# Trainium2: reordering the end of the dense stage and of the last token pair, and operand sums moved to GpSimd, in a fused attention, dense and routed-expert kernel

## The chip, the cores and the metric

The kernel runs on one core of one Trainium2 chip. The metric is the device time of one execution in microseconds (us). The times of before are the median of three runs; the profile comes from one more execution, whose own time stands beside its span below. Engines are named PE (TensorE, matmuls), ScalarE or ACT, VectorE or DVE, GpSimd or POOL, and SyncE or SP, whose queue issues most of the DMAs.

## The reference

```python
def reference(q, k, v, moe..., moe2...):
    # attention: 4 batches, 8 heads, 576 positions, 64 per head;
    # heads 0-3 see the last 32 positions, heads 4-7 every 32nd
    x = attention(q, k, v)                       # 2304 x 512
    gate = 1.0 / (1.0 + np.exp(-(x @ w_gate)))   # w_gate, w_val: 512 x 1536
    x = (gate * (x @ w_val)) @ w_out             # w_out: 1536 x 512
    # routed experts: 8 of them, w1 512 x 1024, w2 1024 x 512
    do_compute = (x @ w_skip) > 0
    xc = x[do_compute]
    e_idx = np.argmax(xc @ w_gate2, axis=1)      # one expert a token
    for e in range(8):
        y[e_idx == e] = gate_w * (np.maximum(xc[e_idx == e] @ w1[e], 0.0) @ w2[e])
    out = x.copy(); out[do_compute] = xc + y
```

The attention's inputs are float32, and the products are held to float32 accuracy: the kernel splits an operand into a high half, rounded for the fast matmul, and a low half, the rest.

## The kernel before, in words

The 2304 tokens are six units of 384 (`UT`), taken in three pairs p = 0, 1, 2 (`NP`). There are four stages.

1. **Attention**, up to about 130 us of the span. Its output leaves in transposed tiles `x`.

2. **Dense stage**, about 131 to 397 us. Gate and value matrices are multiplied in `NC` = 12 chunks of weights (f), for each pair p, by a seven-product scheme for 2 x 2 blocks (Strassen-Winograd): sums of weight blocks (S1 to S4) meet sums of token blocks (T1 to T4). A `Block(f, p)` is one such set of seven products of six matmuls, 128 x 384 each; `mm3` (L593 to L595) makes a product of split operands from three matmuls: high x high, high x low, low x high. The partial sums stand in PSUM banks psA, psB, psC and psD. `period` is the order of one block: it is a generator whose steps mix the products of the block with the end of the block before (`prev`). At its start ScalarE copies psB of the block before into psC (`onto`, L632) and into a temporary (`keep`, L625), and the last products of that block add onto psC. VectorE adds psD onto temporaries (`add_d`, L639) and multiplies gate by value (L655, L658, L666, L670); DMAs store the results in the DRAM tensors `gts` (gT, gB), partly accumulating from GpSimd's queue (L644, L646).

   Work beside the blocks sits in job queues for VectorE ("D"), ScalarE ("A") and GpSimd ("P"). Each step of a period calls `background`, which takes jobs from each queue up to a credit (`RATES`, in us a step) by the jobs' given costs; `need` forces a job and those that it depends on when a product needs its operand. Jobs are: token sums (`combine`, L417; on VectorE for pair 2 in the kernel before), the high half (ScalarE, L429) and low half (VectorE, L433) of token operands, the conversion of weights from 64-bit to 32-bit floats (`convert`, VectorE's L460, L464, L469 and L489, ScalarE's L478), the weight sums (L520) and the split of weights (`split_w`: high halves `wh` on ScalarE, L534; low halves `wl` on VectorE, L537). `out_weights(i)` does the same for a chunk of w_out into a box `wof` and, for every second chunk, makes the weight sums (L576 to L585) and stores all of them in DRAM (wS, wA). The raw weights are fetched one after another in the order of the list `raws_left`; each finished conversion asks for the next (`more_raw`).

   In the last block the operands of the first output steps (`wt["A11", g]`, xt[2], xt[0], xt[1], `wt["A12", 0]`) are loaded and queued as split jobs, and the queues are emptied before `period(None, prev)` ends the last block.

3. **Output projection**, about 397 to 546 us: `NSTEP` = 63 steps k, 21 a pair, three for each of the seven products P1 to P7 in the order of `PROD`. Step k loads the token tile five steps ahead (`load_x`, L970) and weight tiles (`load_w`, L977); ScalarE casts the high half three steps ahead (L984), VectorE subtracts the low half two steps ahead (L992). `finish` splits the sums of a unit's half; `turn_back` turns them with matmuls into rows of tokens (PE L1085 and L1086, ScalarE's row copy L1087, VectorE's L1088 for the routing logits lp); `pick(u)` chooses each token's expert (L1115 to L1125, result oh_all) and stores its rows into the output; `place(u, rank_sums)` ranks the tokens of each expert with small matmuls (L1047 to L1050) and scatters rows to the experts' slots (xs). `at(k, generator, n)` puts n pieces of such work into step k. For the last pair, unit 4 is picked and placed, and unit 5 turned, picked and placed, in straight code after step 62, between the first tiles of expert 0 (`hide`, `hidden`, L1438 to L1442).

4. **Routed experts**, to the end: `hidden_wide` and `outputs_wide` for experts 1 to 7, and for expert 0 `hidden` and `outputs` (L1505 to L1514). GpSimd makes some low halves of expert weights there (L1168).

Instructions are issued in program order on each engine; tiles of one pool tag are reused in turn, and a tile's new writer waits for its old readers.

Of the kernel before, what the change touches and what calls it, by code (L numbers as in the profile page):

```python
# [16 lines left out]
ALU = mybir.AluOpType  # L17
# [6 lines left out]
def kernel(  # L24
# [14 lines left out]
    nc = tc.nc  # L39
    B, H, S, D = q.shape  # L40
# [370 lines left out]
    def combine(p, nm, eng, parts, cost):  # L411

        e = nc.gpsimd if eng == "P" else nc.vector
        for part in parts:
            def fn(part=part):
                x, y = (source(p, z)[:, part, :] for z in SUMS[nm])
                e.tensor_tensor(source(p, nm)[:, part, :], x, y, op=ALU.subtract)  # L417
            before = [sum_job[p, z] for z in SUMS[nm] if z[0] == "T"]
            sum_job[p, nm] = Job(eng, cost, fn, before)
# [317 lines left out]
    def run(steps, n=99):  # L737
        for _ in range(n):
            if next(steps, 0) == 0:
                return  # L740
# [150 lines left out]
    raws_left = []  # L891
    for f in range(2, NC):
        raws_left += [(f, "g"), (f, "v")] + [(i, "o") for i in outs_of[f - 1]]
    raws_left += [(NC - 1, "o")]

    def more_raw():
        if raws_left:
# [7 lines left out]
        operand(1, nm, WHOLE, 0.8, 0.9)  # L905
    split_w(1, *c1)
    for nm in ("T3", "T2", "T4"):
        combine(2, nm, "D", WHOLE, 0.95)
    for nm in OPS:
        operand(2, nm, WHOLE, 0.8, 0.9)  # L910
        if nm in ("T3", "T2", "T4"):
# [26 lines left out]
    def slab2(shape, dt, name):  # L938
        return late.tile(shape, dt, tag="slab2", bufs=NBIG, name=name)

    PROD = (("P1", "A11", "B11", "A"), ("P2", "A12", "B21", "A"), ("P6", "S2", "T2", "B"), ("P7", "S3", "T3", "D"),
            ("P5", "S1", "T1", "B"), ("P4", "A22", "T4", "D"), ("P3", "S4", "B22", "B"))
    NSTEP = NP * len(PROD) * NG
    xt = {}
    wt = {}
# [10 lines left out]
    def load_x(n):  # L956
        if not 0 <= n < NSTEP:
            return
        p, r = divmod(n, len(PROD) * NG)
        j, g = divmod(r, NG)  # L960
        src = gts[p, PROD[j][2], g]
        if n < 2 or (n - 2) % (NBIG + 1) == 0:
            get = (raw_w if n < 2 else
                   lambda shape, dt, name: keep.tile(shape, dt, tag="w3", bufs=2, name=name))
            xt[n] = [get([128, 2, UT], F32, f"xt{n}{c}") for c in range(2)]
            for c in range(2):
                nc.sync.dma_start(xt[n][c][:, 1, :], src[:, c, :])
        else:
            xt[n] = slab2([128, 2, 2, UT], F32, f"xt{n}")
            nc.sync.dma_start(xt[n][:, 1], src)  # L970
# [28 lines left out]
    for f, p in BL:  # L999
        if (f, p) == (0, 2):  # L1000
            for nm in OPS:
                for j in x_jobs[2, nm]:
                    need(j)
            weights(2, more_raw)
        if p == 0 and f > 1:
            if f + 1 < NC:
                weights(f + 1, more_raw)
            for i in outs_of[f]:
                out_weights(i, more_raw)
        if (f, p) == (NC - 1, 1):  # L1010
            for i in outs_of[f]:
                need(wo_jobs[i])
            for g in range(NG):
                load_w("A11", g)
            for n in (2, 0, 1):
                load_x(n)
            load_w("A12", 0)
        k = Block(f, p)
        for i, _ in enumerate(period(k, prev)):
            background(RATES)  # L1020
            if rest0:
                rest0.pop()()
            if (f, p, i) == (NC - 1, NP - 1, 0):
                for x in [wt["A11", g] for g in range(NG)] + [xt[2], xt[0], xt[1], wt["A12", 0]]:
                    split_job(x)
        prev = k
    for eng in "AD":
        while queue[eng]:
            need(queue[eng][0])
    for _ in period(None, prev):  # L1030
        pass
    for eng in "PAD":
        while queue[eng]:
            need(queue[eng][0])
# [7 lines left out]
    def rank_sums(oh, tag="Y"):  # L1042
        nb = oh.shape[1]
        pk = bank([RB, nb + 1, NE], tag)
        for m in range(nb):
            for mm in range(m):
                nc.tensor.matmul(pk[:, m, :], lhsT=ones, rhs=oh[:, mm, :], start=(mm == 0), stop=False)  # L1047
            nc.tensor.matmul(pk[:, m, :], lhsT=tri, rhs=oh[:, m, :], start=(m == 0), stop=True)
        for m in range(nb):
            nc.tensor.matmul(pk[:, nb, :], lhsT=ones, rhs=oh[:, m, :], start=(m == 0), stop=(m == nb - 1))  # L1050
        return pk
# [189 lines left out]
    def finish(u, a, sums, k, adds=None):  # L1241

        if k < NSTEP - 4:
            sh, sl = (raw_w([128, 2, UT], F32R, f"s{n}{u}{a}") for n in "hl")
        else:
            both = slab2([128, 2, 2, UT], F32R, f"s{u}{a}")
            sh, sl = both[:, 0], both[:, 1]
        splits[u, a] = sh, sl

        def highs(x):  # L1250
            for c in range(2):
                nc.scalar.copy(sh[:, c, :], x[c])

        def lows(x):
            for c in range(2):
                nc.vector.tensor_tensor(sl[:, c, :], x[c], sh[:, c, :].bitcast(F32), op=ALU.subtract)

        if adds:
            for c in range(2):
                nc.vector.tensor_tensor(adds[c], adds[c], sums[c], op=ALU.add)  # L1260
            at(k + 1, do(lambda: (highs(adds), after_act.append(lambda: lows(adds)))))
        else:
            highs(sums)
            if k + 1 < NSTEP:
                after_act.append(lambda: lows(sums))
            else:
                lows(sums)
# [9 lines left out]
    def at(k, gen, n=1):  # L1277
        side.setdefault(k, []).append((gen, n))
# [43 lines left out]
    for p in range(NP):  # L1322
        b, ua, ub = PER * p, 2 * p, 2 * p + 1
        last = p == NP - 1
        ta = [later(lambda u=ua, a=a: turn_back(u, a)) for a in range(2)]
        tb = [later(lambda u=ub, a=a: turn_back(u, a)) for a in range(2)]
        for k in range(8, 11):
            at(b + k, ta[0])
        for k in range(17, 20):
            at(b + k, tb[1])  # L1330
        if last:
            at(b + 20, ta[1], 4)
        else:
            for k in range(20, 23):
                at(b + k, ta[1])
        if last:
            break
        for k in range(23, 26):
            at(b + k, tb[0])
        for u, k0 in ((ua, 23), (ub, 27)):  # L1340
            g = later(lambda u=u: pick(u))
            for k in range(k0, k0 + 3):
                at(b + k, g, 3)
            g = later(lambda u=u: place(u, rank_sums(rst[u][1])))
            for k in range(k0 + 3, k0 + 6):
                at(b + k, g, 2)
# [21 lines left out]

    banks, keeps = {}, {}

    def unit(p, j, d, g):

        name, wn, xn, t = PROD[j]
        ps, w, x = banks[t][d], wt[wn, g], xt[PER * p + NG * j + g]
        for c in range(2):
            ds_ = slice(128 * d, 128 * d + 128)
            xhi, xlo = ((x[c][:, i, :] for i in range(2)) if isinstance(x, list) else (x[:, i, c, :] for i in range(2)))
            first, end = g == 0 and c == 0, g == NG - 1 and c == 1
            mm3(ps, w[:, 0, c, ds_].bitcast(F32R), w[:, 1, c, ds_].bitcast(F32R), xhi.bitcast(F32R), xlo.bitcast(F32R),
                first and name in ("P1", "P7"), end, True)  # L1380

# [15 lines left out]
    for p in range(NP):  # L1397
        for t in "ABD":
            banks[t] = [bank([128, UT], t) for d in range(2)]
        if p == 0:  # L1400
            for ps in banks["B"]:
                nc.tensor.matmul(
                    ps, lhsT=wt["A11", 0][:, 0, 0, 0:128].bitcast(F32R), rhs=xt[0][0][:, 0, :].bitcast(F32R),
                    start=True, stop=True)
        for j, (name, _, _, _) in enumerate(PROD):
            wide = name in ("P1", "P2")
            for g in range(NG):
                k = PER * p + NG * j + g
                ahead(k)
                flush(after_act)  # L1410
                two = [divmod(2 * g + i, NG) for i in range(2)] if wide else [(0, g), (1, g)]
                for d, x in two:
                    unit(p, j, d, x)
                    if name == "P1" and x == NG - 1:
                        nc.scalar.copy(banks["B"][d], banks["A"][d])
                for gen, n in side.get(k, ()):
                    run(gen, n)
            after(p, name, k)
# [152 lines left out]
    def hide(*fs):  # L1571
        for f in fs:
            hidden(f, w, pp, hts, 0, HEAD)()

    grab()
    grab()
    hide(0)
    evict = hidden(1, w, pp, hts, 0, HEAD)
    run(pick(NU - 2))
    run(turn_back(NU - 1, 0))  # L1580
    evict()
    run(place(NU - 2, rank_sums(rst[NU - 2][1])))
    run(pick(NU - 1))
    hide(2)
    evict = hidden(3, w, pp, hts, 0, HEAD)
# [168 lines left out]
```

## Time and profile before

| | us |
|---|---|
| median of 3 runs (lowest to highest) | 746.56 (746.31 to 746.75) |
| the profiled execution's own time | 746.6 |
| its span | 744.8 |
| PE busy | 708.6 (95%) |
| VectorE busy | 561.4 (75%) |
| ScalarE busy | 452.1 (61%) |
| GpSimd busy | 258.7 (35%) |

The profile's times count from the start of the span. A timeline row gives start, duration, engine, line, operation, the tile written and the tiles read, shape, and in square brackets the idle time of the engine ahead of the row with what ended it. A row of waits gives waiting engine, line and tile, then the releaser, then the sum of the waits in us, how many, and the longest. PE's granted clock stands in windows as a share of full speed: 1.00 is 2.4 GHz and 0.50 is 1.2 GHz.

### The profile page before, as it was taken

To read this page: it belongs to the slowest core of one execution; us is meant where nothing else is said; L and a number is where in the kernel's file an instruction comes from. 1 tells how busy PE (TensorE), PEld (TensorE's weight loads), DVE (VectorE), ACT (ScalarE), POOL (GpSimd) and SP (SyncE) were. 2 spreads that over 40 slices of the span, in tenths; PEclk is the share of its full clock that TensorE was granted. 3 is DMA by queue.
4 is the path that set the end of the run, shared out by engine and by line. 5 is a ranking of instruction groups with operands and counts; after the bars stand their busy time and mean duration, and the time that the engine had idled before them with its cause. 6 is when DMAs were issued, how large, how long until landed. Compare 5 with 4: busy or idle time off the path is not lost. (4 is left out here: it accounts for less than half of the span.)

```text
span 744.8 us, 14549 instructions
## 1 busy us (share of the span) xinstructions
PE 708.6 (95%) x4783; PEld 663.7 (89%) x4785; DVE 561.4 (75%) x1246; ACT 452.1 (61%) x1206; POOL 258.7 (35%) x289
## 2 busy tenths in 40 slices
PE   8999988999999999999988999999989999999992
PEld 5766666999999999999988999999989899999991
DVE  4799997989988888888866766677865666666650
ACT  5888986755555555555454856565645666676730
POOL 6677876021030211204042000402415644566611
PEclk9999999999999999999998999999998999999997
DMA  9999610397897888979599996779845577677610
GB/s 201 238 208 209 157 41 30 109 256 196 272 222 251 210 233 220 228 256 208 171 293 336 356 326 203 247 235 319 302 162 183 179 238 246 225 246 232 223 38 14
DMA packets 136858, 158.57 MB, mean 213 GB/s; under 512 B 60511, under 2 KB 105823, under 8 KB 136777
## 3 DMA queue, kind: packets, MB, share of 16 engines
q1 hardware_dynamic: 122072, 134.51, 58.4%
q0 software_dynamic: 11936, 19.66, 13.0%
q10 hardware_dynamic: 2768, 3.41, 1.3%
q8 instruction: 40, 0.66, 0.4%
q14 instruction: 42, 0.34, 0.2%
HBM read 103.49 MB, written 59.65 MB: 219 GB/s over the span
## 5 line engine op out<-in xcount | busy, mean ns | idle before, releaser
L644 POOL DMA_DIRECT2D gT<-sC x36 | 31.9, 1030 | 171.1 <-DVE sC L658 137.2
L301 ACT ACTIVATE sm<-psX,mx 96x128 f32<-96x128 f32 (+2 forms) x176 | 61.9, 376 | 10.0 <-DVE mx L295 7.9
L314 POOL TENSOR_TENSOR sm<-sm,rs 96x384 f32<-96x384 f32 (+2 forms) x64 | 55.5, 885 | 31.1 <-DVE rs L308 16.2
L984 ACT CAST xt<-xt 128x768 fp32r<-128x768 f32 (+1 forms) x74 | 53.9, 743 | 18.6 <-DMA xt<-gB 10.4
L992 DVE TENSOR_TENSOR xt<-xt 128x768 fp32r<-128x768 f32 (+1 forms) x74 | 60.4, 831 | 5.8 <-ACT xt L984 5.7
L639 DVE TENSOR_TENSOR u<-psD,u 128x384 f32<-128x384 f32 x70 | 38.6, 552 | 19.0 <-PE psD L595 18.7
L593 PE MATMUL psD<-xhT,wh 128*128 128x384 f32 x140 | 47.3, 338 | 1.5 <-DVE u L639 1.5
L595 PE MATMUL psA<-xhB,wl 128*128 128x384 f32 x140 | 47.0, 336 | 1.3 <-DVE wl L537 1.3
L595 PE MATMUL psD<-xhT,wl 128*128 128x384 f32 x140 | 47.4, 338 | 0.3 <-DVE wl L537 0.3
L594 PE MATMUL psD<-xlT,wh 128*128 128x384 f32 x140 | 47.2, 337 | 0.0
L593 PE MATMUL psA<-xhB,wh 128*128 128x384 f32 x140 | 46.8, 334 | 0.0
L595 PE MATMUL psB<-xhT,wl 128*128 128x384 f32 x140 | 46.8, 334 | 0.0
L594 PE MATMUL psA<-xlB,wh 128*128 128x384 f32 x140 | 46.8, 334 | 0.0
L593 PE MATMUL psB<-xhT,wh 128*128 128x384 f32 x140 | 46.8, 334 | 0.0
L594 PE MATMUL psB<-xlT,wh 128*128 128x384 f32 x140 | 46.8, 334 | 0.0
L632 ACT COPY psC<-psB 128x384 f32<-128x384 f32 x35 | 16.3, 465 | 43.4 <-PE psB L595 43.4
L1521 POOL DMA_INDIRECT out_dram<-xg x16 | 15.3, 957 | 77.2 <-DVE xg L1520 66.4
L625 ACT COPY u<-psB 128x384 f32<-128x384 f32 x70 | 33.9, 484 | 11.2 <-PE psB L595 10.9
L1119 POOL COPY row<-lm_all 128x8 f32<-128x8 f32 x18 | 6.9, 424 | 94.4 <-DVE lm_all L1115 94.4
L301 ACT ACTIVATION_READ_ACCUMULATOR sm<-psX,mx 96x1 f32 (+2 forms) x176 | 38.3, 218 | 0.0
L593 PE MATMUL psB<-xt,wtS 128*128 128x384 f32 x108 | 36.9, 341 | 0.0
L594 PE MATMUL psB<-xt,wtS 128*128 128x384 f32 x108 | 36.3, 336 | 0.6 <-DVE xt L992 0.6
(793 smaller groups left out, 2553.1 us busy)
## 6 DMA issues: line engine op xcount, KB each, us to landing
w1r<-in_moe_w_dram SPq DMA_DIRECT2D x28, 512.0 KB
w2r<-in_moe_w_dram SPq DMA_DIRECT2D x28, 512.0 KB
xt<-gT SPq DMA_DIRECT2D x30, 384.0 KB
gT<-u SPq DMA_DIRECT2D x54, 192.0 KB
xt<-gB SPq DMA_DIRECT2D x22, 384.0 KB
gT<-sC POOLq DMA_DIRECT2D x36, 192.0 KB, 5.9
gB<-sA SPq DMA_DIRECT2D x33, 192.0 KB
wg<-in_moe_w_gate_dram SPq DMA_DIRECT2D x12, 512.0 KB
```

The costliest lines, as they stand in the source:

```text
L301: nc.scalar.activation(sm[:n, w, 0:c], src[:, w, :], AF.Exp, bias=mx[:n, w:w + 1], accum_out=sums[:n, h, w:w + 1])
L314: nc.gpsimd.tensor_tensor(x, x, rs[:n, h, 0:m].rearrange("p (w o) -> p w o", o=1).to_broadcast([n, m, c]), op=ALU.mult)
L593: nc.tensor.matmul(ps, lhsT=whi, rhs=xhi, start=start, stop=False, skip_group_check=skip)
L594: nc.tensor.matmul(ps, lhsT=whi, rhs=xlo, start=False, stop=False, skip_group_check=skip)
L595: nc.tensor.matmul(ps, lhsT=wlo, rhs=xhi, start=False, stop=stop, skip_group_check=skip)
L625: nc.scalar.copy(self.tm[nm], self.ps["B"])
L632: nc.scalar.copy(ps, self.ps[src])
L639: nc.vector.tensor_tensor(self.tm[nm], self.ps["D"], self.tm[nm], op=ALU.add)
L644: nc.gpsimd.dma_start(dst, t, accum_op=ALU.add)
L984: nc.scalar.copy(h.bitcast(F32R), l)
L992: nc.vector.tensor_tensor(l.bitcast(F32R), l, h, op=ALU.subtract)
L1521: ins = nc.gpsimd.indirect_dma_start(out=out[:, :], out_offset=bass.IndirectOffsetOnAxis(ap=xg[t][:n, TW - 1:TW].bitcast(I32), axis=0), in ...
```

## The change

- `raws_left`: the last four raw weights are fetched in the order output chunk 9, gate 11, value 11, output chunk 10 and then output chunk 11; in block (10, 0) `out_weights(9)` is queued ahead of `weights(11)`, and chunk 10 behind it.
- The sums T3, T2 and T4 of pair 2 are made by GpSimd, whole tiles of 128 x 768, with a cost of 1.8 instead of 0.95 in the job queue.
- In the last block only the A11 tiles and xt[2] are queued as split jobs. The splits of xt[0], xt[1] and `wt["A12", 0]` stand between the steps of the closing period: after its first step, after three more and at its end. The bank copy of L632 comes ahead of them.
- The first product P1 of the output projection takes its k-slices in the order 2, 0, 1.
- The last pair's products: P4 ahead of P5 (`PRODS`). P4's finish (step 56) makes its additions and high halves at once. Unit 4 is turned back in steps 58 and 59 and picked in steps 60 to 62; unit 5's second half is turned in step 62. After step 62, `place(4)` follows the first `hide(0)`, ahead of `hidden(1)` and of unit 5's turn.

```diff
-    raws_left += [(NC - 1, "o")]
+    raws_left[-4:] = [raws_left[i] for i in (-2, -4, -3, -1)] + [(NC - 1, "o")]
...
     for nm in ("T3", "T2", "T4"):
-        combine(2, nm, "D", WHOLE, 0.95)
+        combine(2, nm, "P", WHOLE, 1.8)
...
+    PRODS = [PROD] * (NP - 1) + [PROD[:4] + (PROD[5], PROD[4]) + PROD[6:]]
...
         if p == 0 and f > 1:
+            if f == NC - 2:
+                out_weights(outs_of[f][0], more_raw)
             if f + 1 < NC:
                 weights(f + 1, more_raw)
-            for i in outs_of[f]:
+            for i in outs_of[f][f == NC - 2:]:
                 out_weights(i, more_raw)
...
-                for x in [wt["A11", g] for g in range(NG)] + [xt[2], xt[0], xt[1], wt["A12", 0]]:
+                for x in [wt["A11", g] for g in range(NG)] + [xt[2]]:
                     split_job(x)
...
-    for _ in period(None, prev):
-        pass
+    tail = period(None, prev)
+    for n, x in ((1, xt[0]), (3, xt[1]), (9, wt["A12", 0])):
+        run(tail, n)
+        high(x)
+        low(x)
...
-        if adds:
+        if adds and k == NSTEP - 7:
+            for c in range(2):
+                nc.vector.tensor_tensor(adds[c], adds[c], sums[c], op=ALU.add)
+            highs(adds)
+            after_act.append(lambda: lows(adds))
+        elif adds:
...
-        for k in range(17, 20):
-            at(b + k, tb[1])
-        if last:
-            at(b + 20, ta[1], 4)
-        else:
+        if not last:
+            for k in range(17, 20):
+                at(b + k, tb[1])
+        if not last:
             for k in range(20, 23):
                 at(b + k, ta[1])
         if last:
+            for k, n in ((16, 1), (17, 2)):
+                at(b + k, ta[1], n)
+            g = later(lambda: pick(ua))
+            for k in range(18, 21):
+                at(b + k, g, 3)
+            at(b + 20, tb[1], 4)
             break
...
-                    unit(p, j, d, x)
+                    unit(p, j, d, (x + 2) % NG if k < NG else x, x)
...
     hide(0)
+    run(place(NU - 2, rank_sums(rst[NU - 2][1])))
     evict = hidden(1, w, pp, hts, 0, HEAD)
-    run(pick(NU - 2))
     run(turn_back(NU - 1, 0))
     evict()
-    run(place(NU - 2, rank_sums(rst[NU - 2][1])))
     run(pick(NU - 1))
```

Three places where the order of instructions changes follow. The first is GpSimd's queue at the start of the dense stage; xT are token sums, the L644 rows are the accumulating stores of the first block. A piece of the difference:

```order
 L417 TENSOR_TENSOR xT_2256<-x_963,xT_2154 128x384
 L417 TENSOR_TENSOR xT_2364<-x_2029,x_1498 128x384 x2
-L644 DMA gT_00_86<-sC_2612 128x384
-L644 DMA gT_00_83<-sC_2612 128x384
-L644 DMA gT_00_89<-u_10_2533 128x384
+L417 TENSOR_TENSOR xT_2421<-x_2030,x_2029 128x768
+L417 TENSOR_TENSOR xT_2454<-x_2030,xT_2364 128x768
+L417 TENSOR_TENSOR xT_2474<-x_1499,xT_2454 128x768
```

The three sums of pair 2 are new in this queue and stand ahead of the first block's stores; on VectorE they stood right behind the two subtractions L537 of chunk 1.

The second is ScalarE at the end of the dense stage, from the gate's sigmoid of the last block on; xt and wtA are the tiles that come from DRAM. Before:

```order
L636 ACTIVATE sA_5210<-psA 128x384
L984 CAST xt_5073<-xt_5073 128x384
L984 CAST xt_5074<-xt_5074 128x384
L984 CAST xt_5077<-xt_5077 128x384
L984 CAST xt_5078<-xt_5078 128x384
L984 CAST wtA_5081<-wtA_5081 128x512
L632 COPY psC<-psB 128x384
L625 COPY u_112_5237<-psB 128x384
```

Now:

```order
L636 ACTIVATE sA_5210<-psA 128x384
L632 COPY psC<-psB 128x384
L625 COPY u_112_5227<-psB 128x384
L985 CAST xt_5073<-xt_5073 128x384
L985 CAST xt_5074<-xt_5074 128x384
L636 ACTIVATE sC_5240<-psC 128x384
L985 CAST xt_5077<-xt_5077 128x384
L985 CAST xt_5078<-xt_5078 128x384
L985 CAST wtA_5081<-wtA_5081 128x512
```

The bank copy and the addend's copy moved ahead of the five casts (L984, which is L985 in the changed file).

The third is PE after the last output step; L1438 to L1442 are a hidden tile of expert 0 (L1454 to L1458 in the changed file), L1085 the turn of unit 5 and L1048 the rank sums (L1054). Before, from the end of the first hidden tile on:

```order
L1442 MATMUL psY<-xx_6992,we03l 128x128
L1438 MATMUL psY<-xx_6992,we03h 128x256
L1438 MATMUL psY<-xx_6992,we00h 128x256
L1440 MATMUL psY<-xx_6992,we00l 128x128
L1438 MATMUL psY<-xx_6992,we01h 128x256
L1440 MATMUL psY<-xx_6992,we01l 128x128
L1438 MATMUL psY<-xx_6992,we02h 128x256
L1440 MATMUL psY<-xx_6992,we02l 128x128
L1442 MATMUL psY<-xx_6992,we03l 128x128
L1438 MATMUL psY<-xx_6992,we03h 128x256
L1085 MATMUL psY<-wri,s_7040 128x148
```

Now:

```order
L1458 MATMUL psY<-xx_7007,we03l 128x128
L1454 MATMUL psY<-xx_7007,we03h 128x256
L1054 LDWEIGHTS tri
L1054 MATMUL psY<-oh_all,tri 128x8
L1053 LDWEIGHTS ones
L1053 MATMUL psY<-oh_all,ones 128x8
```

The rank sums of unit 4 stood behind unit 5's turn and stand right behind the first hidden tile now.

## Rows read from the trace of the kernel before

**Rows 1.** The page, busy us, share of the span, instructions, per engine

```profile
PE 708.6 (95%) x4783; PEld 663.7 (89%) x4785; DVE 561.4 (75%) x1246; ACT 452.1 (61%) x1206; POOL 258.7 (35%) x289
```

**Rows 2.** PE's waits: releaser, sum in us, times, longest

```profile
PE psC L593 <- ACT psC L632: 4.2, 1, 4.2
...
PE psD L593 <- DVE u L639: 1.5, 1, 1.5
PE psY L1048 <- DVE oh_all L1125: 1.4, 1, 1.4
...
PE psB L594 <- DVE xt L992: 0.6, 1, 0.6
...
PE psD L595 <- DVE wl L537: 0.3, 1, 0.3
```

**Rows 3.** PE's timeline, end of the dense stage

```profile
388.29 0.33 PE L594 MATMUL psB<-xlT,wh 128*128 128x384 f32 x1
388.46 0.34 PE L595 MATMUL psB<-xhT,wl 128*128 128x384 f32 x1
393.00 0.69 PE L593 MATMUL psC<-xhB,wh 128*128 128x384 f32 x1 [4.21 <-ACT psC L632]
393.49 0.52 PE L594 MATMUL psC<-xlB,wh 128*128 128x384 f32 x1
...
398.61 0.41 PE L593 MATMUL psA<-xt,wtA 128*128 128x384 f32 x1
```

**Rows 4.** ScalarE's timeline, same place

```profile
391.95 0.62 ACT L984 CAST wtA<-wtA 128x512 fp32r<-128x512 f32 x1 [0.50 <-DMA wtA<-wA]
392.48 0.47 ACT L632 COPY psC<-psB 128x384 f32<-128x384 f32 x1
```

**Rows 5.** Windows: length, each engine's busy us, PE's clock, DMA share, GB/s

```profile
410.00:420.00 10.00, 10.00 (x62) 10.00 (x61) 7.25 (x12) 8.23 (x16) 0.00 (x0) 1.00 0.96 326
...
430.00:440.00 10.00, 9.98 (x61) 9.76 (x59) 6.51 (x10) 4.91 (x8) 0.00 (x0) 1.00 1.05 368
...
444.00:450.00 6.00, 5.84 (x36) 5.66 (x36) 5.48 (x14) 4.05 (x10) 0.00 (x0) 1.00 0.39 126
```

**Rows 6.** ScalarE's timeline, output projection

```profile
434.09 0.83 ACT L984 CAST xt<-xt 128x768 fp32r<-128x768 f32 x1 [2.39 <-DMA xt<-gB]
```

**Rows 7.** VectorE's timeline, ahead of block (11, 0)

```profile
364.95 0.43 DVE L460 TENSOR_SCALAR wof<-wo 128x512 int32<-128x512 int32 x1 [1.89 <-DMA wS<-wof]
```

**Rows 8.** VectorE's timeline, start of the dense stage

```profile
129.95 0.77 DVE L351 COPY x<-psY 128x108 f32<-128x108 f32 x2 [1.14 <-PE psY L339]
...
136.26 0.96 DVE L537 TENSOR_TENSOR wl<-stage,wh 128x768 fp32r<-128x768 f32 x1 [0.25 <-ACT wh L534]
137.59 1.22 DVE L537 TENSOR_TENSOR wl<-stage,wh 128x1024 fp32r<-128x1024 f32 x1 [0.37 <-ACT wh L534]
...
140.07 1.94 DVE L417 TENSOR_TENSOR xT<-x,xT 128x768 f32<-128x768 f32 x2
```

**Rows 9.** GpSimd's timeline, end of the attention stage

```profile
123.39 1.32 POOL L417 TENSOR_TENSOR xT<-x,xT 128x384 f32<-128x384 f32 x1
124.79 1.98 POOL L417 TENSOR_TENSOR xT<-x,x 128x384 f32<-128x384 f32 x2
```

**Rows 10.** Timelines of GpSimd and VectorE, 104 to 107 us

```profile
104.38 1.73 POOL L314 TENSOR_TENSOR sm<-sm,rs 96x384 f32<-96x384 f32 x2 [1.07 <-ACT kq L258]
...
104.13 0.51 DVE L433 TENSOR_TENSOR xlT<-xT,xhT 128x384 fp32r<-128x384 f32 x1
...
105.03 1.50 DVE L433 TENSOR_TENSOR xlT<-xT,xhT 128x384 fp32r<-128x384 f32 x1
```

**Rows 11.** PE's timeline, after the last output step

```profile
556.95 0.18 PE L1048 MATMUL psY<-oh_all,tri 128*128 128x8 bf16 x1 [1.41 <-DVE oh_all L1125]
```

**Rows 12.** Windows, same columns, expert 0

```profile
559.00:566.00 7.00, 7.00 (x27) 6.12 (x27) 2.71 (x10) 3.73 (x10) 4.53 (x10) 0.51 0.28 106
```

**Rows 13.** Waits of the DMA queue on SP, 382 to 444 us

```profile
SPq L970 <- PE psB L595: 8.5, 6, 2.6
```

More of the change, by code (lines that the diff above doesn't have):

```diff
@@ L960, in load_x @@
         j, g = divmod(r, NG)
-        src = gts[p, PROD[j][2], g]
+        src = gts[p, PRODS[p][j][2], g]
         if n < 2 or (n - 2) % (NBIG + 1) == 0:
@@ L1369, with unit @@
     banks, keeps = {}, {}
-    def unit(p, j, d, g):
-        name, wn, xn, t = PROD[j]
+    def unit(p, j, d, g, i):
+        name, wn, xn, t = PRODS[p][j]
         ps, w, x = banks[t][d], wt[wn, g], xt[PER * p + NG * j + g]
@@ L1376, in unit @@
             ds_ = slice(128 * d, 128 * d + 128)
-            xhi, xlo = ((x[c][:, i, :] for i in range(2)) if isinstance(x, list) else (x[:, i, c, :] for i in range(2)))
-            first, end = g == 0 and c == 0, g == NG - 1 and c == 1
+            xhi, xlo = ((x[c][:, z, :] for z in range(2)) if isinstance(x, list) else (x[:, z, c, :] for z in range(2)))
+            first, end = i == 0 and c == 0, i == NG - 1 and c == 1
             mm3(ps, w[:, 0, c, ds_].bitcast(F32R), w[:, 1, c, ds_].bitcast(F32R), xhi.bitcast(F32R), xlo.bitcast(F32R),
@@ L1404 @@
                     start=True, stop=True)
-        for j, (name, _, _, _) in enumerate(PROD):
+        for j, (name, _, _, _) in enumerate(PRODS[p]):
             wide = name in ("P1", "P2")
```

## The prediction

> **What bounds the kernel now.** I began with the page: PE is busy for 95% of the span, VectorE for 75% [rows 1]. So time can be gained only where PE waits or where its clock is down, and it is lost wherever PE is made to wait. The waits of PE, sorted by what ended them, name the places [rows 2]: 4.2 us once for the bank copy of L632, 1.5 us once for the addition of L639, 1.4 us once for oh_all of L1125.
>
> The 4.2 us stand at the end of the dense stage [rows 3]: PE's last matmul into psB starts at 388.46, the next one at 393.00, and then at half speed. From 393.49 to 398.61 sixteen matmuls follow one another at 0.32 us, where 388.29 to 388.46 shows 0.17. That is 16 x 0.15 + 0.3 (the first one, 0.49 instead of 0.17) = 2.7 us more. The place costs 4.2 + 2.7 = 6.9 us. ScalarE's timeline shows why [rows 4]: the copy stands behind five casts, each of which waits for a load from DRAM or for the one before it (391.95, after a wait of 0.50, is the last); it runs at 392.48 although its input was complete before 389.
>
> **The change, part by part.** All sums are against the profiled execution (span 744.8, its own time 746.6; the median of the runs, 746.56, is 0.04 below it). A difference below 0.2%, 1.5 us, can't be told from no change.
>
> *Bank copy first.* The copy and the addend's copy no longer stand behind casts that wait for DMA. At the place itself it leaves some 0.5 us (the eviction of 0.47 us in [rows 4] and its handover), so 6.9 - 0.5 = 6.4 us come free at 389. The question is whether they arrive at the end. The windows [rows 5] say no: the DMA engines are busy for a share of 0.96 to 1.05 in the stretches shown up to 440 (those around them, from 382 to 444, read alike) and 0.39 after 444. In that stretch ScalarE, two to three output steps ahead of PE, already waits 2.4 us at once for a tile [rows 6], and PE itself 0.6 us for one [rows 2]. An earlier PE reaches those tiles earlier, and they come no sooner. What can be kept is the free share, 10 x (1 - 0.96) = 0.4 us, and PE's own 0.6 us, which comes from the row copies that ScalarE has to do between PE's steps: 1.0 us. The bounds are 0 and 6.4; I take -1.0, since the row of the full DMA engines is the nearest.
>
> *Weight chunk 9 earlier.* VectorE's L460 at 364.95 had waited 1.89 us for the store of the previous box [rows 7]; behind it in VectorE's queue stands the addition on which PE's 1.5 us end [rows 2]. Now chunk 9 is converted a block earlier, its stores have a block's time, and wof10 finds its box free. What remains is the usual handover, 0 to 0.3 us: I take -1.3, bounds 0 and -1.5. The low halves of chunk 11 come later on VectorE than before; PE needs them a block further on, so I cost that at nothing. If this cover is gone, PE waits for wl there, by up to the 1.2 us of one such subtraction [rows 8].
>
> *Three operand sums on GpSimd.* VectorE loses three instructions of 0.95 us (140.07 shows two in 1.94 [rows 8]), which stand behind the low halves wl that PE waits for at this time; PE's wait here was 0.3 us [rows 2], so nothing is to be gained but that. GpSimd takes 1.98 us for two halves [rows 9], so some 2.0 us for each whole tile, 2.6 if it meets VectorE as at 123.39 (1.32 for one half). The price lies elsewhere: at 104.13 a subtraction with two SBUF inputs takes VectorE 0.51 us, at 105.03 the same takes 1.50 us and ends just after GpSimd's two L314, 104.38 to 106.11 [rows 10]. VectorE stood still while GpSimd ran. The first sum can start at 130.7 (L351, begun at 129.95, copies its last input [rows 8]), the other two after the low halves of earlier operands are done, that is among VectorE's close row up to 138.8 and not behind it. By hand: the first holds VectorE for 1.1 us, the second for nearly 2.0 ahead of the first wl, the third for some 1.5 ahead of the second; the two wl end 2.8 and 4.3 us later than at 136.26 + 0.96 = 137.2 and 137.59 + 1.22 = 138.8 [rows 8]. PE uses them at once and has no reserve. I take +4.0; the lower end is -0.3 (the sums fall into gaps of VectorE), the upper 7.8 (three sums of 2.6 us, each of which holds VectorE for its whole length). The store issues behind the sums on GpSimd's queue are late by up to 10 us, and none is read before 382: no cost.
>
> The Trainium skill, "SBUF — State Buffer", section "Who interferes with whom", says that the port pair shared by VectorE and GpSimd is an exclusive lock, and that whoever comes second waits for the whole instruction. This trace agrees (1.50 instead of 0.51). By that rule VectorE can also come first and GpSimd wait, which is the cheap case, rival 1.
>
> *Last pair.* P4 ahead of P5 lets unit 4 be turned back and chosen during steps 58 to 62; its rank sums then stand right behind the first hidden tile, and VectorE's placing of unit 4 is done before unit 5's choice begins. PE's wait for oh_all, 1.41 us at 556.95 [rows 11], was for unit 5's choice behind unit 4's placing, six short instructions: I take 1.0 of it for these and leave 0.4 (bounds 0 and 1.4). The shorter waits around it stay. After those waits the clock falls: 0.51 in 559 to 566 [rows 12], that is 7.0 x 0.49 = 3.4 us. With less waiting I expect it to stay up; it stayed up after the single 1.5 us at 366 and fell after the 4.2 us, and this is between. So -1.0 - 3.4 = -4.4; the bounds are 0 (no choice comes earlier and the clock falls) and -1.4 - 3.4 = -4.8.
>
> *The rest.* The order of the k-slices in P1, moved output stores and the swapped products P4 and P5 move equal work: 0.
>
> Sum: -1.0 - 1.3 + 4.0 - 4.4 = -2.7, so 746.6 - 2.7 = **743.9 us**.
>
> **Rivals.**
> 1. *GpSimd's sums cost nothing.* They start in VectorE's gaps, or VectorE comes first. For it: VectorE's two short waits for ScalarE at this place, 0.25 and 0.37 us [rows 8]. Against: [rows 10]. Then +4.0 becomes 0: 739.9.
> 2. *The loads follow the earlier PE.* The share near 1 is partly waiting inside the DMA engines, and the loads could be issued earlier when PE frees the buffers earlier. For it: the queue of the loads waits for PE to free buffers in that stretch, 8.5 us in six waits [rows 13]. Against: the share of 0.96 to 1.05 in spite of these waits, at 368 GB/s in 430 to 440 [rows 5]. Then -1.0 becomes -6.4: 738.5.
> 3. *The clock falls in the tail all the same.* -4.4 becomes -1.0: 747.3, no change that can be told. For it: the waits that stay around that place.
> 4. *Slower: GpSimd locks VectorE in full.* Three sums of 2.6 us, 7.8 us, all ahead of the second wl; PE waits as long, and as after the 4.2 us its clock falls, 2.7 us by [rows 3]. Then +10.5 in place of +4.0: 750.4. It decides from +8.2 on (746.6 - 6.7 + 8.2 = 748.1). Against: VectorE's instructions stand close together, and GpSimd has to find its turn.
> 5. *The copy doesn't come first after all.* If ScalarE's queue had kept a cast in front, the 6.9 us would stay; the order of the instructions speaks against it, and since only 1.0 of it counts, it would give 744.9. It is inside my forecast's own spread.
>
> **How the numbers follow.** The forecast with the spread of its terms (742.4 to 745.4) gets 0.42, with 0.03 of that above 745.1. Rival 1 gets 0.17, rival 2 0.12, both clearly faster. Rival 3 gets 0.17, of which 0.03 comes with a cheaper GpSimd term and so is faster. Rival 4 gets 0.12. Faster by over 0.2%: 0.39 + 0.17 + 0.12 + 0.03 = 0.71, less 0.01 for rival 5: 0.70. Within 0.2%: 0.03 + 0.14 + 0.01 = 0.18, slower 0.12. The range reaches down to rival 2 and up past rival 3: 738.0 to 748.0; outside are most of rival 4 and the case in which rivals 1 and 2 hold together (733).
>
> **What would show it.** Right: no wait of PE for L632 at the end of the dense stage, but several waits of 0.5 to 2.5 us for xt tiles in steps 13 to 20 that add up to over 4 us; PE's wait for L639 at 366 gone; waits of PE for wl between 137 and 144 of 3 to 5 us, with a VectorE subtraction of 2 us or more beside a GpSimd L417; the clock at 1.00 around 560. Wrong: if PE's waits for wl stay below 1 us (rival 1), if output step 20 starts over 3 us earlier than the dense stage's other terms move it (rival 2), if the clock reads 0.5 near 560 (rival 3), or if a stretch of half clock stands after 140 (rival 4). The forecast fails as a whole if the half clock turns up at a place where it was full before, behind the new waits for xt.

## The result, and the profile after

The changed kernel is slower: 754.21 us (median of 4 runs, 752.9 to 756.38) against 746.43 us for the kernel before in the same comparison, ratio 1.0109 with a 95% interval of 1.0081 to 1.0138. Two later comparisons of the same two kernels gave 1.0075 (1.0054 to 1.0096) and 1.0063 (1.0029 to 1.0097). The forecast was 743.9 us, in a range that ended at 748.0.

The times of one kernel spread by some microseconds, mostly along with the granted clock of the run (in the last comparison the changed kernel took 749.98 to 751.53 us in its five runs at 0.985 to 0.987 and 752.29 to 754.89 us in the seven at 0.976 to 0.981), so each verdict below is a ratio of many runs and each profile is one draw; the one in this section is that of the 756.38 us.

The page of the changed kernel, busy time by engine, and PE's waits (engine, line and tile, releaser, then us in total, how many, longest):

```profile
PE 714.0 (95%) x4785; PEld 668.6 (89%) x4785; DVE 562.5 (75%) x1243; ACT 452.1 (60%) x1206; POOL 264.8 (35%) x292
```

```profile
PE psA L595 <- DVE wl L537: 3.2, 2, 1.9
PE psA L593 <- ACT psB L1431: 3.1, 1, 3.1
...
PE psD L595 <- DVE wl L537: 1.4, 1, 1.4
PE psB L593 <- DVE v L1271: 1.2, 1, 1.2
PE psD L593 <- DVE u L639: 1.0, 1, 1.0
...
PE psD L593 <- ACT v L1283: 0.7, 1, 0.7
...
PE psC L593 <- ACT psC L632: 0.6, 1, 0.6
```

Read beside [rows 2]: the bank copy's 4.2 us are 0.6, the 1.5 us at 366 are gone (the 1.0 us for u is at another place, 393.8), and so is the 1.4 us wait for oh_all. All three waits that the change aimed at did go. But new ones have come, of which these five are the main ones: 1.9 and 1.4 us for wl (the other 1.3 us of the first line stood in the trace before as well), 3.1 us for another bank copy (L1431), 0.7 us for v out of psD and 1.2 us for the sum of v.

The same instructions of PE in both traces show where the time went (start, duration, then what ended the idle time). Before:

```profile
168.54 0.44 PE L595 MATMUL psA<-xhB,wl 128*128 128x384 f32 x1 [1.31 <-DVE wl L537]
...
397.65 0.52 PE L593 MATMUL psA<-xt,wtA 128*128 128x384 f32 x1
...
443.74 0.44 PE L594 MATMUL psB<-xt,wtS 128*128 128x384 f32 x1 [0.59 <-DVE xt L992]
...
548.18 0.33 PE L1438 MATMUL psY<-xx,we00h 128*128 128x256 f32 x1
```

After:

```profile
173.35 0.44 PE L595 MATMUL psA<-xhB,wl 128*128 128x384 f32 x1 [1.31 <-DVE wl L537]
...
391.55 0.34 PE L595 MATMUL psB<-xhT,wl 128*128 128x384 f32 x1
...
396.33 0.33 PE L593 MATMUL psA<-xt,wtA 128*128 128x384 f32 x1
...
449.59 0.45 PE L594 MATMUL psB<-xt,wtS 128*128 128x384 f32 x1 [0.91 <-DVE xt L993]
...
556.68 0.33 PE L1454 MATMUL psY<-xx,we00h 128*128 128x256 f32 x1
```

PE is 4.8 us late after the moved sums (173.35 - 168.54), 3.1 us late ahead of the bank copy (391.55 against 388.46 in [rows 3]), 1.3 us **early** at the first output step (396.33 against 397.65), 5.8 us late in output step 20 (449.59 against 443.74), 8.5 us late at the first tile of expert 0 and 9.8 us at the end of the span (754.6 against 744.8). So in this pair of traces chunk 9 gave 1.7 us and the bank copy 4.4 us; the sums took 4.8, the first twenty output steps 7.1, the last pair and expert 0 another 4.0 us.

The start of the dense stage, VectorE and GpSimd of the changed kernel:

```profile
131.72 1.38 DVE L655 SCALAR_TENSOR_TENSOR sC<-sC,u 128x384 f32<-128x384 f32 x1
...
135.82 2.61 DVE L433 TENSOR_TENSOR xlT<-xT,xhT 128x768 fp32r<-128x768 f32 x1
138.35 3.71 DVE L537 TENSOR_TENSOR wl<-stage,wh 128x768 fp32r<-128x768 f32 x2
```

```profile
130.84 1.85 POOL L417 TENSOR_TENSOR xT<-x,x 128x768 f32<-128x768 f32 x1 [4.02 <-DVE x L351]
135.18 2.43 POOL L417 TENSOR_TENSOR xT<-x,xT 128x768 f32<-128x768 f32 x1 [2.49 <-DVE xlT L433]
138.57 2.41 POOL L417 TENSOR_TENSOR xT<-x,xT 128x768 f32<-128x768 f32 x1 [0.96 <-DVE xlT L433]
```

Each of GpSimd's three rows lies under a row of VectorE that is too long: 1.38 for some 0.55 us, 2.61 for 0.95, and 3.71 for the two wl, 0.96 + 1.22 in [rows 8]. The third sum ends at 140.98 and the second wl at 142.06, one subtraction later. PE's rows say what that cost:

```profile
139.35 0.44 PE L595 MATMUL psA<-xhB,wl 128*128 128x384 f32 x1 [1.90 <-DVE wl L537]
...
142.12 0.60 PE L595 MATMUL psD<-xhT,wl 128*128 128x384 f32 x1 [1.44 <-DVE wl L537]
142.51 0.52 PE L593 MATMUL psD<-xhT,wh 128*128 128x384 f32 x1
142.83 0.52 PE L594 MATMUL psD<-xlT,wh 128*128 128x384 f32 x1
```

That is 1.90 + 1.44 us of waiting, 3.1 more than the 0.28 before, and then steps of 0.32 us (142.51 to 142.83): the clock is at its half level for the next stretch (0.78 of full speed as the mean of 140 to 144 us, 0.79 from 144 to 148), which costs 4 x 0.22 + 4 x 0.21 = 1.7 us and makes the 4.8.

The end of the dense stage, ScalarE of the changed kernel, answers to [rows 4]:

```profile
391.98 0.46 ACT L632 COPY psC<-psB 128x384 f32<-128x384 f32 x1 [1.48 <-PE psB L595]
...
402.51 0.83 ACT L985 CAST xt<-xt 128x768 fp32r<-128x768 f32 x1 [6.32 <-DMA xt<-gB]
...
404.54 0.83 ACT L985 CAST xt<-xt 128x768 fp32r<-128x768 f32 x1 [0.16 <-DMA xt<-gB]
405.28 0.47 ACT L1431 COPY psB<-psA 128x384 f32<-128x384 f32 x1
```

The first bank copy waits for PE alone now. The next one, from psA to psB at the end of P1, stands behind the casts of xt tiles 3 and 4, and the first of these waits 6.3 us for its load. It is the same pattern as before, one bank copy further on. PE loses 3.1 us there, and in this trace the clock is down behind it (0.65 in the window of 403 to 410 us, 1.00 before).

### The profile page after: what moved, and what is told of

Read it like the earlier page. It is cut to its first block, busy times and chain, and to the rows that moved or that the text cites. A ratio compares the mean times of both kernels' runs of the same rounds, so it can differ in the third digit from the quotient of the medians.

```text
span 754.6 us, 14553 instructions
## 1 busy us (share of the span) xinstructions
PE 714.0 (95%) x4785; PEld 668.6 (89%) x4785; DVE 562.5 (75%) x1243; ACT 452.1 (60%) x1206; POOL 264.8 (35%) x292
## 5 line engine op out<-in xcount | busy, mean ns | idle before, releaser
L644 POOL DMA_DIRECT2D gT<-sC x36 | 31.8, 1025 | 160.3 <-DVE sC L658 152.9
L985 ACT CAST xt<-xt 128x768 fp32r<-128x768 f32 (+1 forms) x74 | 53.8, 743 | 25.8 <-DMA xt<-gB 13.9
L639 DVE TENSOR_TENSOR u<-psD,u 128x384 f32<-128x384 f32 x70 | 38.7, 553 | 20.5 <-PE psD L595 20.2
L632 ACT COPY psC<-psB 128x384 f32<-128x384 f32 x35 | 16.3, 465 | 46.2 <-PE psB L595 46.2
```

The source lines that it names most:

```text
L632: nc.scalar.copy(ps, self.ps[src])
L639: nc.vector.tensor_tensor(self.tm[nm], self.ps["D"], self.tm[nm], op=ALU.add)
L644: nc.gpsimd.dma_start(dst, t, accum_op=ALU.add)
L985: nc.scalar.copy(h.bitcast(F32R), l)
```

## The experiments

The four parts of the change were measured alone, then the whole without one part, then the mechanisms.

### Each part alone

**Only the sums.**

```diff
     for nm in ("T3", "T2", "T4"):
-        combine(2, nm, "D", WHOLE, 0.95)
+        combine(2, nm, "P", WHOLE, 1.8)
```

> Only the three operand sums moved to GpSimd. Theory A (each part's price is its own, as read from the milestones of the two traces): PE waits for wl, 3.1 us more than before in two waits near 137 and 140 us, and a half-clock stretch near 142 costs 1.7 us: +4.8 us, and nothing is won back. Theory B (the delay is absorbed by the loads that limit the output projection): PE is 4.8 us late at 172 us, but less than 2 us at the end.

Measured: 1.0072 (1.0055 to 1.0089), so 5.4 us slower. PE's waits for wl are again 1.90 and 1.46 us. Theory A holds (its 4.8 us lie in the interval, 4.1 to 6.6 us); the loads absorb nothing that can be told.

**Only chunk 9** (`raws_left` and `out_weights(9)` ahead of `weights(11)`).

> Only weight chunk 9 fetched and converted earlier. Theory A: PE's 1.5 us wait for L639 near 366 us goes, and the time falls by 1.5 to 1.7 us. Theory B: the loads of the output projection start no earlier, and PE waits as much longer at L632 or for xt: within 0.5 us of before.

Measured: 0.9962 (0.9948 to 0.9977), 2.8 us faster, which is more than the 1.5 us wait. PE's wait for L639 is gone. Theory A, if anything by more than it asked: the interval reaches down to 1.7 us, the removed wait and a little. In this profile L632 costs 3.7 us instead of 4.2.

**Only the bank copy**, with P1's slice order.

```diff
-                for x in [wt["A11", g] for g in range(NG)] + [xt[2], xt[0], xt[1], wt["A12", 0]]:
+                for x in [wt["A11", g] for g in range(NG)] + [xt[2]]:
...
+    tail = period(None, prev)
+    for n, x in ((1, xt[0]), (3, xt[1]), (9, wt["A12", 0])):
+        run(tail, n)
+        high(x)
+        low(x)
```

> Only the bank copy ahead of the casts, with P1's slices in the order 2, 0, 1. Theory A: the 4.2 us at L632 fall to about 1.6 us in all, PE reaches the fourth output step over 4 us earlier, waits there some 3 us for the copy of psA behind a cast that waits for its load, and the clock is at half for 6.8 us after that instead of before: 1 to 3 us slower. Theory B (the loss at this place in the changed kernel came with the 3 us by which its earlier stage was late): 1 to 2 us faster.

Measured: 0.9991 (0.9965 to 1.0017), no change. Neither theory's sign: nothing is lost and nothing kept. PE's waits say why:

```profile
PE psD L593 <- DVE u L639: 2.6, 2, 1.6
PE psA L593 <- ACT psB L1418: 2.6, 1, 2.6
...
PE psY L1089 <- DVE sl L1259: 0.8, 1, 0.8
...
PE psC L593 <- ACT psC L632: 0.6, 1, 0.6
```

The 4.2 us have become 0.6 (L632), 1.0 (the second of the waits for u, for VectorE's subtractions of xt tiles), 2.6 (L1418, the copy of psA) and 0.8.

**Only the last pair** (`PRODS`, the finish of P4, unit 4 chosen in steps 60 to 62, placed behind `hide(0)`).

> Only the last pair: P4 ahead of P5, unit 4 chosen in the output steps, placed behind the first hidden tile. Theory A: two new waits, 0.7 us at the start of P4 for the copy out of psD and 1.2 us at the start of P3 for the addition from psB, and the half clock after them stands for 13.7 instead of 6.8 us: 2 to 4 us slower. Theory B (the long stretch of half clock came from the waits earlier in the changed kernel or by chance): the clock is at half for 6.8 us or not at all, and the time is between 2 us faster and 0.5 us slower.

Measured: 1.0007 (0.9972 to 1.0042), with single runs from 742.74 us (mean granted clock 0.990) to 750.67 (0.979). PE's new waits in the profiled run:

```profile
PE psB L593 <- DVE v L1266: 1.2, 1, 1.2
PE psD L593 <- ACT v L1278: 1.0, 1, 1.0
```

Theory A's waits are there, and behind them its long half clock: 0.50 in the window of 552 to 559 us and 0.59 in that of 559 to 566, 14 us against the 7 of [rows 12]. The time lies at the edge of theory B's range, and its interval reaches into theory A's. From output step 30 to the first tile of expert 0 PE takes 82.7 us here and 79.7 in the trace before, 2.9 us more; by the measured +0.5 us the earlier choice of unit 4 gives some 2.4 of them back later (an estimate).

### The whole without one part

**The changed kernel again**, on another chip than its parts.

> The changed kernel itself, beside its parts. Theory A (the parts add up as measured alone: the sums +5.4 us, chunk 9 -2.8, the bank copy -0.7, the last pair between -1 and +3): 3 to 6 us slower than before. Theory B (the parts hurt one another through the clock, which falls after more of the waits): over 6 us slower, as in the first measurement.

Measured: 1.0075 (1.0054 to 1.0096), 5.6 us: theory A's range. But the parts alone add up to 5.4 - 2.8 - 0.7 + 0.5 = +2.4 us, and the whole lies 2 to 6 us above that in its three comparisons. Since the four intervals together leave the sum open by some 4 us either way, a surplus is likely and not shown. Part of it may be the clock: up to 700 us the trace of the first comparison stands at half clock for 24 us, those of the second and third for 10 each and that of the kernel before for 14, and 10 us at half clock cost some 5.

**Without the sums.**

> The changed kernel with the three operand sums back on VectorE. Theory A (the sums alone make the change slow): 1 to 4 us faster than before, 5 us and more faster than the changed kernel. Theory B (the rest is slow together, by the waits at the fourth output step and in the last pair and the clock after them): 0 to 3 us slower than before.

Measured: 0.9967 (0.9944 to 0.9990), 2.5 us faster than before. By theory A's numbers: with the sums on VectorE the rest of the change is a gain, about that of chunk 9 alone, and the sums make the whole slow: 1.0075 / 0.9967 = 1.0108 for them here.

**Chunk 9 and the bank copy.**

> Weight chunk 9 earlier and the bank copy first, nothing of the last pair and of the sums. Theory A (the loads set the end of this stretch, the bank copy is worth nothing): as chunk 9 alone, 2 to 3 us faster than before. Theory B (the bank copy pays once the stage before it has no wait): 4 us and more faster.

Measured: 0.9960 (0.9945 to 0.9975), as chunk 9 alone. The bank copy is worth nothing here either. PE's waits between 385 and 450 us:

```profile
PE psA L593 <- ACT psB L1420: 1.6, 1, 1.6
PE psD L593 <- DVE u L639: 1.0, 1, 1.0
PE psB L594 <- DVE xt L992: 0.9, 1, 0.9
PE psY L1091 <- DVE sl L1261: 0.8, 1, 0.8
PE psY L1090 <- ACT sh L1257: 0.8, 1, 0.8
PE psC L593 <- ACT psC L632: 0.6, 1, 0.6
```

Together 5.7 us of small waits where one of 4.2 and one of 0.6 us stood.

**Without the last pair, without the bank copy, and the whole once more**, in one comparison.

> The change without its part on the last pair. Theory A (the sums and the last pair together make the tail's waits and its long half clock): 0.2 to 0.5% slower than before. Theory B (the sums' delay makes the bank copy lose): 0.8% and more slower, as the whole.

> The change without the bank copy first and without P1's new slice order. Theory A: as the whole, 0.7 to 1.1% slower than before. Theory B (the bank copy loses with the sums): 0.2 to 0.5% slower.

> The changed kernel again, beside the two that leave one part out. Both theories: 0.7 to 1.1% slower than before; what tells them apart is which of the two others is clearly below it.

Measured: 1.0030 (0.9986 to 1.0075), 1.0048 (1.0008 to 1.0088) and 1.0063 (1.0029 to 1.0097). The intervals overlap, and neither part is shown to add to the price of the sums (1.0072 alone, 1.0108 in the whole). Whether anything does stays open.

### The mechanisms

**The sums behind the wl tiles.** A small GpSimd copy that reads the second wl tile stands ahead of the sums.

```diff
+    def touch():
+        t = small.tile([128, NE], F32, tag="ex", bufs=2, name="touch")
+        nc.gpsimd.tensor_copy(t, wl[1, 1][:, 0, 0:NE].bitcast(F32))
+
+    behind.append(Job("P", 0.1, touch, [w_jobs[1][-1]]))
```

> The three sums on GpSimd, but behind a small GpSimd copy that reads the second wl tile of chunk 1, so that none of them runs before VectorE has made both wl tiles. Theory A (the price is that GpSimd holds VectorE while PE waits for wl): PE's two waits for wl near 138 and 140 us go back to 0.3 us in all, VectorE is held later, where PE has reserve, and the time is within 1 us of before. Theory B (the price is the sums' own length, whenever they run): 3 us and more slower still, with waits of PE for xh or xl tiles.

Measured: 1.0041 (1.0026 to 1.0056), 3.1 us slower. PE's waits for wl near 138 and 140 are down to 0.26 us, as theory A says, but the time is theory B's. Other waits stand in their place, and not for the xh or xl tiles that theory B names: 0.7 us for u of ScalarE and 1.7 us for u of VectorE, at 145 and 148. GpSimd's first sum here and the VectorE row beside it:

```profile
139.97 1.84 POOL L419 TENSOR_TENSOR xT<-x,x 128x768 f32<-128x768 f32 x1
```

```profile
140.05 2.58 DVE L435 TENSOR_TENSOR xlB<-x,xhB 128x768 fp32r<-128x768 f32 x1 [0.29 <-ACT xhB L431]
```

The subtraction lasts until 142.63, 0.82 us beyond the end of the sum: it did its work after it. So the hold went along with the sums to this second place, and VectorE has no reserve a few us later either.

**Idle sums, first try.** Six GpSimd subtractions of 128 x 384 that nobody reads, all sums of the kernel on VectorE as before.

```diff
+    def idle_sum():
+        t = late.tile([128, UT], F32, tag="idle", bufs=1, name="idle")
+        nc.gpsimd.tensor_tensor(t, source(2, "B22")[:, 0, :], source(2, "B12")[:, 0, :], op=ALU.subtract)
+
+    for _ in range(6):
+        Job("P", 0.7, idle_sum)
```

> The kernel before, all its sums on VectorE, and in addition six GpSimd subtractions of 128x384 at the place of the three moved sums; their result is read by nobody and nothing waits for them. Theory A (GpSimd holds VectorE): VectorE's two-input subtractions beside them take 1.5 us and more instead of 0.95, both wl tiles come late, PE waits 2 to 5 us for wl between 137 and 142 us, and the time rises by 2 to 5 us. Theory B (the late results of the sums are what is waited for): no wait of PE above 0.5 us there, and the time of before within 1 us.

Measured: 1.0011 (0.9998 to 1.0025). Inconclusive: their inputs are complete earlier than those of the moved sums, so they ran from 126.6 to 133.5 us and were over before VectorE came to the wl tiles; PE's wait there was 0.8 us. VectorE was held here too: its L655 and L658 beside them took 1.12 and 1.37 us instead of 0.55, at a place where that cost little.

**Idle sums, second try,** each pair reading what the moved sums had waited for.

```diff
+    for c in range(2):
+        Job("P", 0.9, lambda c=c: idle_sum(lambda: source(2, "B22")[:, 1, :], lambda: source(2, "B12")[:, 1, :]))
+    for nm in ("T1", "T4"):
+        for c in range(2):
+            Job("P", 0.9, lambda nm=nm, c=c: idle_sum(lambda: xl[1, nm][:, c, :].bitcast(F32),
+                                                      lambda: source(2, "B12")[:, 1, :]), x_jobs[1, nm])
```

> The kernel before, all its sums on VectorE, and six idle GpSimd subtractions of 128x384, which nobody waits for, placed as the moved sums ran: two after x is complete, two after the low half of T1 and two after that of T4, each pair reading that low half. Theory A (GpSimd holds VectorE): VectorE's subtractions for T4's low half and for wl take 1.5 us and more, PE waits 1.5 us and more for wl in all, the time rises by 1.5 to 5 us. Theory B (the late results are what is waited for): PE's wait for wl stays under 0.5 us and the time within 1 us of before.

Measured: 1.0111 (1.0032 to 1.0189), from four runs of 748.79 to 760.12 us; the trace is that of the lowest. VectorE, GpSimd and PE of this kernel:

```profile
137.87 3.69 DVE L537 TENSOR_TENSOR wl<-stage,wh 128x768 fp32r<-128x768 f32 x2
```

```profile
135.53 6.89 POOL L912 TENSOR_TENSOR idle<-xlT,x 128x384 f32<-128x384 f32 x4 [2.02 <-DVE xlT L433]
```

```profile
139.67 0.44 PE L595 MATMUL psA<-xhB,wl 128*128 128x384 f32 x1 [1.92 <-DVE wl L537]
```

Nobody waits for these four GpSimd rows, and the two wl take 3.69 us as in the changed kernel (3.71); PE waits 1.92 us for the first as there (1.90). For the second it waits 0.21 us and not 1.44, since its clock has fallen by then (0.57 in 140 to 144 us) and it comes later itself. Theory A: VectorE held by GpSimd is enough for the wait, without a late result; how much of the time it explains, the wide interval leaves open (2.4 to 14.1 us). VectorE holds GpSimd in turn, 6.89 us for four subtractions of about 1.0.

**The loads.** The 13 zero stores to xs (260 KB each) move from steps 9 to 15 to steps 18 to 24, first with chunk 9 and the bank copy, then with chunk 9 alone, then with ScalarE's copies of psA ahead of the casts of xt tiles 4 and 5.

```diff
-    for k in range(9, 16):
+    for k in range(18, 25):
         at(k, gx)
```

> Chunk 9 earlier and the bank copy first, as measured together before, and the 13 zero stores to xs (260 KB each) moved from output steps 9 to 15 to steps 18 to 24, behind the stretch in which the DMA engines are full. Theory A (the loads bound the output projection's start, and the bank copy's gain is lost to them): PE's waits for xt and for the row copies between 430 and 443 us shrink to under 0.5 us, and the time is 1.5 to 4 us below that of chunk 9 with the bank copy, so 0.6 to 0.9% below before. Theory B (the wait at the fourth step, before any zero store, is what loses it): same as chunk 9 with the bank copy, 0.4% below before.

> Chunk 9 earlier and the zero stores late, with the bank copy where it was before. Theory A (PE is late enough there to find its tiles, so the loads do not bound it): as chunk 9 alone, 0.3 to 0.4% below before. Theory B (the loads bound the kernel before as well): 0.6% and more below.

> As the one with the zero stores late, and in addition ScalarE's two copies of psA to psB at the end of P1 stand ahead of the casts of xt tiles 4 and 5. Theory A (the wait at the fourth output step is a copy behind a cast that waits for its load): that wait, 1.6 us, falls under 0.5 us, and the time falls by a further 0.5 to 1.5 us. Theory B (the tile itself comes late): the wait stays, now for xt, and the time is the same.

Measured against before: 0.9919 (0.9899 to 0.9938), 0.9943 (0.9921 to 0.9966) and 0.9933 (0.9915 to 0.9952). The first is 740.39 us, the best of all, 6.0 us below before and more below the changed kernel. That is what theory A asks for: PE's small waits between 430 and 443 us are gone, and so are the full DMA engines of [rows 5] (same columns):

```profile
420.00:430.00 10.00, 10.00 (x61) 10.00 (x60) 8.04 (x13) 8.73 (x17) 0.00 (x0) 1.00 0.84 265
430.00:440.00 10.00, 10.00 (x62) 10.00 (x61) 8.70 (x16) 5.17 (x10) 0.00 (x0) 1.00 0.80 232
```

From output step 12 to step 30 PE now takes 42.4 us instead of the 46.3 of chunk 9 with the bank copy; with chunk 9 alone the stores' move is worth only 42.7 against 42.4 there. So the loads did take from an early PE. The second run's time comes out between its two theories, and its interval overlaps that of the first, so how much of the gain needs the bank copy is not settled.

The traces show that the copy's gain is lost at a second place, ahead of all zero stores. The same matmul of the fourth step in the first, second and third run:

```profile
401.95 0.45 PE L593 MATMUL psA<-xt,wtA 128*128 128x384 f32 x1 [3.36 <-ACT psB L1420]
```

```profile
401.41 0.33 PE L593 MATMUL psA<-xt,wtA 128*128 128x384 f32 x1
```

```profile
398.88 0.44 PE L593 MATMUL psA<-xt,wtA 128*128 128x384 f32 x1 [0.38 <-ACT psB L1420]
```

With the copy first, PE begins the output steps 3.0 us earlier than without (392.19 against 395.17), and here it is 0.5 us behind. In the third run the wait of 3.4 us fell to 0.4, 0.3 and 0.6, the last two for xt, as theory A asks, and in its trace PE begins step 30 at 462.83, 1.0 us ahead of the second. The time is the same as that of the first, as theory B asks (741.17 us against 740.39, intervals that overlap). Which of the two holds stays open.

## Why the prediction was wrong

**The place of the bank copy, and that the loads take its gain: right.** Forecast -1.0, measured alone 0.9991, -0.7 us with an interval that holds both. The wait at L632 went, waits came back in the load-bound stretch, and they went with the zero stores. I put all of the new waits into steps 13 to 20; the largest came at step 3, in a copy behind a cast, and it cost 2.6 us alone and 1.6 us with chunk 9 before that stretch begins. The prediction had that pattern before it, in [rows 4], and did not look for the next copy in the same queue.

**Chunk 9: right, mis-sized.** Forecast -1.3, measured -2.8 (-1.7 to -3.9).

**The sums: right in mechanism, mis-sized.** The step "the two wl end 2.8 and 4.3 us later" measured 138.35 + 3.71 - 138.81 = 3.3 us for the second, and PE lost 3.1 us more in waiting, less than the 4.0 I took. The half clock behind these waits, which I had left to rival 4, adds 1.7 us in the trace above; alone the sums measured 5.4 us. The time came out on rival 4's side (slower), but not by its price: the sums took 1.9 to 2.4 us and not 2.6, and cost half of its 10.5.

**The last pair: wrong, and the largest error.** The step that failed is "the swapped products P4 and P5 move equal work: 0". They do equal work, in banks that are not free. P4 adds onto psD, where P7 has just ended and from which ScalarE must still copy v; P3 adds onto psB, where P5 has just ended and from which VectorE must still add v. In the old order P5 lay between P7 and P4, and P4 between P5 and P3, and covered both. The two waits measured 0.7 to 1.6 and 1.2 us in the traces with the swap. In all six of them PE takes 82.3 to 83.3 us from output step 30 to the first tile of expert 0, and 79.7 in the twelve without, so 2.6 to 3.5 us are lost there before any gain; the two waits make up 1.9 to 2.8 of them. The other 3.4 us of the forecast hung on "with less waiting I expect it to stay up". In the trace above the half clock in the tail lasted 14 us instead of 7:

```profile
559.00:566.00 7.00, 7.00 (x35) 6.96 (x34) 3.88 (x23) 2.06 (x7) 3.67 (x9) 0.50 0.49 158
566.00:573.00 7.00, 7.00 (x44) 6.91 (x44) 3.51 (x18) 2.72 (x9) 3.00 (x3) 0.55 0.61 213
```

In the changed kernel's third comparison it lasted 10 us. In its second it stayed up, with 1.6 and 1.2 us in the same two waits:

```profile
559.00:566.00 7.00, 5.25 (x48) 4.64 (x47) 4.03 (x27) 2.41 (x9) 3.70 (x9) 1.00 0.72 225
```

So it is not shown that the two waits lengthen the half clock, nor that less waiting would have ended it.

Forecast -4.4, measured alone +0.5 (-2.1 to +3.1).

**The sum.** With the measured terms it is +2.4 us and not -2.7, and 4.9 of these 5.1 us are the last pair (the errors of the other three nearly cancel). What then lacks to the whole, 2 to 6 us, belongs to no single part that the runs could tell. The range ended at 748.0 because it left a gain of 1.0 us or more in the last pair in every rival, and gave the half clock only to single rivals, while the runs show it to come and go behind the same waits. In the first trace it came at all three places that the prediction had named as signs of being wrong: after 140, near 560, and at a place where the clock was full before (403 to 410), there behind the new wait for the copy and not for an xt tile. In the trace of the third comparison it came only near 560.

## What to carry to other kernels

Swapping two products of equal length is not free: look up which bank each reads out of or adds onto, and what lay between two uses of one bank. A wait that is taken off the head of an in-order queue can come back at the next instruction that stands behind the same loads, so ask first whether the loads are early enough; here moving stores out of their way was worth 3.0 us with the copy in place (6.0 against 3.0 us below before), and the copy alone nothing that could be told. GpSimd elementwise work beside VectorE's two-input instructions was paid by VectorE here, even when nobody waited for the result; whether that costs time depends on who waits for VectorE just then.

## What the runs showed of the hardware

The price of a wait in clock was not fixed. The same two waits for wl, 1.9 and 1.4 to 1.5 us, stand in several profiles; in two of them the windows 140 to 144 and 144 to 148 us read as follows, first for the changed kernel without the bank copy, then for the changed kernel in its third comparison (columns as above, the clock ahead of the last two):

```profile
140.00:144.00 4.00, 2.54 (x9) 2.23 (x9) 4.00 (x5) 1.94 (x3) 0.66 (x1) 0.74 0.00 0
144.00:148.00 4.00, 4.00 (x20) 4.00 (x20) 2.27 (x4) 2.69 (x6) 0.00 (x0) 0.83 0.67 221
```

```profile
140.00:144.00 4.00, 2.56 (x15) 2.24 (x14) 4.00 (x4) 1.94 (x3) 0.85 (x1) 1.00 0.00 0
144.00:148.00 4.00, 4.00 (x25) 4.00 (x24) 3.71 (x6) 3.44 (x6) 0.00 (x0) 1.00 0.63 198
```

In the one the clock fell to 0.74 and 0.83 of its full level, that is 4 x 0.26 + 4 x 0.17 = 1.7 us, in the other it stayed at 1.00. The changed kernel's second comparison, with waits of 1.9 and 1.1 us, read 0.59 and 0.56, so 4 x 0.41 + 4 x 0.44 = 3.4 us. A forecast for such a place needs these cases, with a chance for each.
